# Sliding-window attention and a gated convolution FFN: another order table, batch 0's band masks as TensorE matmuls, conv taps dealt anew

## The chip, the cores and the metric

One core of one Trainium2 chip. The metric is the device time of one execution in microseconds (us), the median of several. Executions of this kernel scatter by 1 to 2%, so each is marked fast or slow (slow: more than 1.5% above the fastest run of the same kernel), and only fast ones are compared. Every ratio below is the mean time of one kernel's fast runs over the mean of the other's fast runs in the same rounds on the same chip, with a 95% interval; it is therefore not quite the ratio of the quoted medians. "Points" are per cent of the time before in such a ratio. A profile is one execution, and its span is some 2 us shorter than the time of the same execution.

## The reference, cut to what matters

```python
# q, k, v: (8 batches, 8 heads, 576 positions, 64)
scores = scale * q @ k.T                    # only |i - j| <= 32 counts
attn = softmax(where(mask, scores, -1e9)) @ v
x = attn.transpose(0, 2, 1, 3).reshape(8, 576, 512)
h = maximum(x @ w_in, 0)                    # 512 -> 1024
conv_out = sum(conv_w[k] * shifted(h, k) for k in range(3))   # along the sequence
out = (h * sigmoid(conv_out)) @ w_out       # 1024 -> 512
```

## The kernel before

The program first writes down all its operations, each with what it reads, writes and which buffers it uses. A table, made by a planner, then fixes in which order they are emitted and on which engine. In `1863S` the number is the operation, the letter the engine: P TensorE, V VectorE, S ScalarE, G GpSimd, D the sync queue, Q ScalarE's own DMA queue; digits behind it choose buffers, and `2F` is two filler matmuls. **Every engine works through its part of the table in order**: if one entry waits, all later entries of the same engine wait.

```python
BUFS = {'st': 3, 'qkb': 5, ..., 'xn': 3, ..., 'y': 7}
CONV = ('33333333', '33q3323r23223321', ...)      # who does the three taps of each unit
ORDER = """15D 11D0 12D 1F 17D ..."""             # 1616 entries
...
def load_v(b, c):                                  # one block of v, 192 or 256 KB, f32
    loader[e].dma_start(vst[..., c, :, :], v[b, :, s0:s1, :]...)
def cast_v(b, c):                                  # to bf16, by V, S or G
    copy(e, ve_b[b % 2][:, c, :, 0:64], vst[:, c, :, :])
...
def emit_exp(e_): scalar.activation(at_..., ps..., AF.Exp, scale=scale)
def emit_mask(e_): (vector if e_ == "V" else gpsimd).tensor_tensor(   # attn * mask
    out=at_..., in0=at_..., in1=mask, op=ALU.mult)
...
# normalised output -> transposed tile, by a transposing transfer ("xd") or by TensorE
loader[e_].dma_start_transpose(to, xn.ap[:, c]...)
```

The parts meet like this: load q, k, v; cast to bf16; transposes and scores on TensorE; exponentials on ScalarE; masks; value products; normalisation; transposed again; first projection (`ph`), relu, three taps, tanh, gate, second projection (`py`), copy `y`, store. Names such as "v 7 4" mean block 4 of v of batch 7.

The softmax here doesn't subtract the row's maximum and nothing guards it: scores larger than these inputs give would overflow.

## Time and profile before

| | before |
|---|---|
| time, median of 3 runs (lowest to highest) | 228.39 us (228.12 to 232.81) |
| span of the profile | 225.6 us |
| TensorE / VectorE / ScalarE / GpSimd busy | 94 / 87 / 83 / 61% |
| mean wait of a transposing transfer from ready to issued | 3.5 us |

TensorE is the bound; how its time adds up is in the prediction. Columns: engine, tile and line, what ended the wait; total us, times, longest.

```profile
POOL ve L232 <- DMA vst<-in_v_dram: 5.8, 6, 1.8
...
ACT ve L232 <- DMA vst<-in_v_dram: 0.7, 1, 0.7
```

These are casts of v that reached the head of their engine's queue before the block had landed. GpSimd (POOL), the engine with the most time to spare, does almost all of that waiting; ScalarE (ACT) waits once, 0.7 us.

### The profile page before, as it was taken

The page shows a single profiled execution, that of the slowest core. Times are in us where ns is not written, and L with a number is a line of the kernel's source. Part 1 is how long each engine was busy: PE and PEld are TensorE (multiplying, and loading weights), DVE is VectorE, ACT ScalarE, POOL GpSimd, SP SyncE. Part 2 cuts the span into 40 slices and gives each one's busy share as a digit, 9 for nine tenths or more (in the row PEclk, how much of TensorE's full clock was granted, in tenths as well). Part 3 has the DMA queues.
Part 4 walks back from the last instruction along what each step waited for, and adds up shares of the span by engine and source line. Part 5 has one row for each costly group of instructions (what it writes and reads, how often), then busy time and mean ns, then how long its engine had stood idle before and what let it go on. Part 6 is the DMA issues. An engine that isn't in the chain of part 4 may idle for free.

```text
span 225.6 us, 7189 instructions
## 1 busy us (share of the span) xinstructions
PE 211.5 (94%) x2720; PEld 122.9 (54%) x2720; DVE 197.3 (87%) x467; ACT 187.5 (83%) x474; POOL 137.7 (61%) x203
## 2 busy tenths in 40 slices
PE   7698899989989999989999998999999999999993
PEld 5366567658555655545555454545655565455541
DVE  6279869899999979797999788989999999899990
ACT  2689899998989889879889989689989999777642
POOL 5978654654376937695368736756386735566640
PEclk9889999999999999999999999999999999999999
DMA  6999999999989999999997989994535212501224
GB/s 201 331 285 358 355 266 281 321 308 253 290 170 324 317 175 287 236 306 224 288 347 129 202 278 358 182 231 147 144 36 118 99 46 49 175 1 49 93 101 178
DMA packets 66391, 48.16 MB, mean 214 GB/s; under 512 B 50781, under 2 KB 50805, under 8 KB 66357
## 3 DMA queue, kind: packets, MB, share of 16 engines
q1 hardware_dynamic: 64992, 46.32, 78.6%
q10 hardware_dynamic: 1364, 1.39, 2.9%
q8 instruction: 21, 0.34, 0.8%
q14 instruction: 14, 0.11, 0.2%
HBM read 32.52 MB, written 9.44 MB: 186 GB/s over the span
## 4 chain that ended last, share of the span: by engine, by line
PE 41%; DVE 18%; ACT 17%; DMA 13%; issue 5%; SPq 3%; POOL 2%; DVEq 0%; ACTq 0%; POOLq 0%
PE pf L232 41%; DMA st<-in_k_dram 7%; ACT attn L232 6%; DVE pf L232 5%; DVE gT L232 4%; SPq L232 3%; DMA out_dram<-y 3%; ACT xn L232 3%; DVE qkT L232 2%; ACT pf L232 2%; DMA vo<-ve 2%; DVE attn L232 2%; DVE xn L232 2%; ACT qkb L232 2%; ACT y L232 1%
## 5 line engine op out<-in xcount | busy, mean ns | idle before, releaser
L232 PE MATMUL pf<-xT,w_in_sb 128*128 128x385 bf16 (+2 forms) x416 | 73.4, 315 | 3.6 <-ACT hT L232 0.9
L232 PE MATMUL pf<-w_out_sb,gT 128*128 128x512 bf16 x288 | 72.2, 380 | 0.0
L232 POOL TENSOR_SCALAR cp<-hT,conv_w_sb 128x384 f32<-128x384 bf16 (+1 forms) x63 | 38.9, 622 | 46.1 <-ACT hT L232 20.2
L232 ACT ACTIVATE pf<-pf 128x384 f32<-128x384 f32 (+1 forms) x104 | 48.2, 477 | 13.1 <-DVE pf L232 11.1
L232 DVE SCALAR_TENSOR_TENSOR gT<-pf,hT 128x384 bf16<-128x384 f32 (+1 forms) x104 | 52.1, 517 | 5.5 <-ACT pf L232 5.1
L232 PEld LDWEIGHTS <-w_in_sb 128*128 128x128 bf16 x416 | 38.6, 98 | 27.8 <-issue 4.5
L232 ACT ACTIVATE attn<-pf 128x512 bf16<-128x512 f32 (+1 forms) x96 | 41.4, 522 | 1.8 <-PE pf L232 1.8
L232 ACT ACTIVATE hT<-pf 128x385 bf16<-128x385 f32 (+2 forms) x76 | 35.4, 487 | 6.0 <-PE pf L232 5.6
L232 PEld LDWEIGHTS <-gT 128*128 128x128 bf16 x288 | 26.0, 98 | 25.7 <-DVE gT L232 0.5
L232 DVE SCALAR_TENSOR_TENSOR pf<-hT,conv_w_sb,pf 128x384 f32<-128x384 bf16 (+1 forms) x61 | 34.7, 586 | 1.2 <-PE pf L232 1.1
L232 PE MATMUL pf<-hT,diag_w 128*128 128x384 bf16 (+1 forms) x153 | 30.9, 309 | 0.9 <-DVE xn L232 0.6
L232 POOL TENSOR_SCALAR qkb<-st 128x1152 bf16<-128x1152 f32 (+1 forms) x23 | 25.7, 1122 | 7.6 <-DMA st<-in_k_dram 3.2
L232 DVE COPY qkT<-pf 128x576 bf16<-128x576 bf16 x35 | 25.6, 750 | 4.9 <-PE pf L232 4.9
L232 POOL TENSOR_TENSOR cp<-cp,cp 128x384 f32<-128x384 f32 (+1 forms) x24 | 24.4, 1016 | 1.6
L232 DVE TENSOR_TENSOR attn<-attn,mask 128x1152 bf16<-128x1152 bf16 x26 | 23.0, 886 | 2.4 <-ACT attn L232 2.3
L232 ACT ACTIVATE xn<-pf,rec 128x64 bf16<-128x64 f32 x96 | 22.0, 360 | 1.5 <-DVE rec L232 1.5
L232 ACT COPY y<-pf 128x512 f32<-128x512 f32 x30 | 18.1, 605 | 3.9 <-PE pf L232 3.7
L232 DVE SCALAR_TENSOR_TENSOR pf<-hT,conv_w_sb,cp 128x384 f32<-128x384 bf16 (+1 forms) x35 | 21.2, 618 | 0.0
L232 POOL TENSOR_TENSOR attn<-attn,mask 128x1152 bf16<-128x1152 bf16 x6 | 14.2, 2371 | 8.4 <-ACT attn L232 8.4
L232 DVE TENSOR_TENSOR xn<-pf,rec 128x256 bf16<-128x256 f32 x48 | 18.9, 410 | 0.0
L232 ACT COPY qkT<-pf 128x576 bf16<-128x576 bf16 x29 | 18.6, 664 | 0.4 <-PE pf L232 0.2
L232 PEld LDWEIGHTS <-diag_w 128*128 128x128 bf16 x153 | 13.3, 97 | 9.8 <-issue 1.3
(49 smaller groups left out, 235.2 us busy)
## 6 DMA issues: line engine op xcount, KB each, us to landing
st<-in_q_dram SPq DMA_DIRECT2D x16, 576.0 KB, 6.8
out_dram<-y SPq DMA_DIRECT2D x36, 256.0 KB, 3.8
st<-in_k_dram SPq DMA_DIRECT2D x14, 576.0 KB, 8.2
vst<-in_v_dram SPq DMA_DIRECT2D x24, 256.0 KB, 7.0
vst<-in_v_dram SPq DMA_DIRECT2D x15, 192.0 KB, 5.7
vo<-ve SPq DMA_DIRECT2D x11, 260.0 KB, 5.6
st<-in_moe_w_in_dram SPq DMA_DIRECT2D x2, 1024.0 KB, 9.3
st<-in_moe_w_out_dram SPq DMA_DIRECT2D x2, 1024.0 KB, 9.4
```

The costliest lines, as they stand in the source:

```text
L232: return lambda *args, **kwargs: fixed(do(*args, **kwargs))
```

## The change

It means to plan the order with an honest issue time for transposing transfers, to take batch 0's masks off the path that starts the FFN (a large negative number is added outside the band by TensorE before the scores accumulate, so that the exponential gives 0), and to deal conv taps and other work to the engines anew.

```diff
+SPLIT = (1,)
-BUFS = {'st': 3, 'qkb': 5, ... 'xn': 3, 'hT0': 8, 'hT1': 6, ... 'gT': 4, 'y': 7}
+BUFS = {'st': 4, 'qkb': 6, ... 'xn': 2, 'hT0': 5, 'hT1': 8, ... 'gT': 3, 'y': 4}
-TURNS = (..., 'edddd')
+TURNS = (..., 'deddd')
+MASKS = ('aa', 'mm', 'mm', 'mm', 'mm', 'mm', 'mm', 'mm')
-CONV = ('33333333', '33q3323r23223321', 's222r32q', ...)
+CONV = ('33333333', '33q3323r23223322', 's222r32r', ...)
-ORDER = """15D 11D0 12D ...          (1616 entries)
+ORDER = """17D 11D0 12D ...          (1607 entries, all drawn anew)
...
+                if added:
+                    for n, e, width in ((2, x, 2), (0, 0, 8), (1, 1, 8)):
+                        rows = slice(64 * e, 64 * e + 64)
+                        tensor.matmul(ps[n].ap[...], outside[rows, :],
+                            ident[rows, None, rows].broadcast_to([64, width, 64]), start=True, stop=False)
...
-                        start=True, stop=True,
+                        start=not added, stop=not (added and more),
```

## The prediction

> **What bounds the kernel now.** I read the busy shares first, then the chain that ended last in order of time, then the busy time by stretch, then TensorE's and the DMA queue's own timelines.
>
> ```profile
> PE 211.5 (94%) x2720; PEld 122.9 (54%) x2720; DVE 197.3 (87%) x467; ACT 187.5 (83%) x474; POOL 137.7 (61%) x203
> ...
> 25.80 7.68 PE pf L232 x93
> ...
> 136.25 48.21 PE pf L232 x603
> ...
> 191.53 2.44 DMA xT<-xn
> 194.01 27.28 PE pf L232 x142
> ```
>
> TensorE is the busiest, VectorE and ScalarE close behind. The real work starts at 25.80 us: the first input projection (`ph`), once batch 0's attention is finished; before that TensorE runs fillers. Two long pieces of the chain are TensorE alone; between 34 and 130 us it changes hands.
>
> ```profile
> 25.80:60.00 34.20, 33.23 (x491) 22.81 (x492) 30.45 (x78) 32.05 (x88) 16.45 (x23) 1.00 1.13 299
> 60.00:110.00 50.00, 47.80 (x764) 26.82 (x763) 45.06 (x105) 44.16 (x110) 34.39 (x32) 1.00 1.08 248
> 110.00:140.00 30.00, 28.12 (x347) 15.78 (x346) 26.96 (x67) 27.08 (x71) 19.61 (x25) 1.00 1.01 275
> 140.00:185.00 45.00, 45.00 (x571) 24.48 (x571) 43.86 (x95) 38.91 (x97) 28.56 (x35) 1.00 0.60 132
> ```
>
> The columns are TensorE, its weight loads, VectorE, ScalarE, GpSimd. TensorE has idle time until 140 us and none from 140 to 185. Its busy time overstates its work[...], so I sum floors, from the step from one start to the next within a group: 0.164 us for 385 columns, 0.163 for 384, 0.216 for 512, and per group 0.36 for 18 transposes, 0.39 for 18 score and 0.13 for 8 value matmuls, 0.22 for a transposed block. After 25.80 that makes 58.1 (88 whole units) + 5.3 (16 half units) + 62.2 (288 output matmuls) + 22.1 (diagonal taps) + 9.7 + 10.9 + 8.2 + 2.2 = **178.7 us**. The stretch from 25.80 to the last matmul's end at 221.7 is 195.9 us, so **about 17 us** are waits and switches. Then 3.9 us for the last copy and store. Span: 25.8 + 178.7 + 17.2 + 3.9 = 225.6; the timed median is 2.8 us more.
>
> ```profile
> 137.80 9.16 SPq L232 DMA_TRANSPOSE xT<-xn  x6
> ...
> 164.67 6.08 SPq L232 DMA_TRANSPOSE xT<-xn  x4
> ...
> 186.20 6.55 SPq L232 DMA_TRANSPOSE xT<-xn  x5
> ```
>
> This is the sync queue's issue time: a transposing transfer holds it 1.3 to 1.5 us in a burst (29 of them sum to 43.6 us, mean 1.50, longest 3.3), an ordinary one 0.5 (median of 120).
>
> [...]
> - [...] 1.5 us of issue against 3.6 us median to landing. That supports planning with a longer issue.
> [...]
>
> **The change, part by part.**
>
> *Batch 0's masks.* Four multiplications leave VectorE and its path. The two that count:
>
> ```profile
> 19.38 0.76 DVE L232 TENSOR_TENSOR attn<-attn,mask 128x1152 bf16<-128x1152 bf16 x1 [0.38 <-ACT attn L232]
> ...
> 20.81 0.74 DVE L232 TENSOR_TENSOR attn<-attn,mask 128x1152 bf16<-128x1152 bf16 x1
> ```
>
> The last value matmuls wait until 21.55, though the last exponential ended at about 19.5: a 2 us path. In their place come 12 mask matmuls, 4 x (2 x 0.216 + 0.056) = 2.0 us, where TensorE would run fillers. But the head is re-dealt too: the taps' diagonal matrices, 8 us on GpSimd, go mostly to VectorE (18 products at about 0.15 us, estimated from the 0.193 us mask copy of that size: 2.7); ScalarE gets the first casts of q and k; batch 0's normalisations all go to VectorE (four left ScalarE, which took 0.8 us each, for 0.33). Walking ScalarE's new queue with measured steps (cast 0.52 or 0.63, eviction 0.53, exponential 0.48 or 0.16; k of batch 0 landing at 8.5 and the second k at 12.55 as before): first scores start at 13.15 instead of 11.4, since the second q's casts now go ahead of them; exponentials end at 19.8. From there VectorE runs 4 reciprocals, 6 products of 0.33, one copy, two block copies of 0.60, to 24.3; the last transposed block and its copy by ScalarE end at 25.4. First projection at **25.45, gain 0.35 us**: of the masks' 2 us most is given back by later scores and a longer VectorE queue.
>
> *Conv kinds.* Diagonal taps on TensorE go from 118 whole + 35 half to 121 + 36: +3 x 0.163 + 0.083 = **+0.6 us** of the bound. GpSimd loses four tap products and two sums (4.8 us), which it had to spare. So this moves work to the bound and gains nothing by count.
>
> *The rest of the deal after the first projection*, count times step: VectorE 171.2 to 174.3 us (+4 relu 1.9, +4 output copies 2.4, +2 block copies 1.2, +3 casts 1.4, -5 q/k evictions 3.3 and small ones); ScalarE 159.2 to 158.8; GpSimd 118.9 to 113.0. VectorE's margin under TensorE shrinks from 7.5 to 5.0 us. Up to chunk 1's last output, ScalarE is dealt 45.9 us against 43.1 before and TensorE's 44.5 in both: that early stretch is ScalarE's.
>
> *Transposing transfers.* In the old order batches 6 and 7 issue them in pairs with no TensorE work between; measured in TensorE work, 11 of 28 steps are under 1.2 us, though each takes 1.5. In the new order 6 are. What it can win directly is small:
>
> ```profile
> who waited for it (us, times):
> ...
>   PE pf L232: 0.8, 2
> ```
>
> These are waits on the transposed tile, 0.5 of them on a transfer. At 192.5 TensorE lost 0.66 us before chunk 10. Indirectly a queue that runs late delays loads and v's shifted copies; at 87.0 TensorE lost 0.5 us for one of those, and the chain passes through the sync queue at 79 to 83 and 107 to 110. The gaps of TensorE over 0.3 us after 25.8 sum to some 6.7 us, most behind VectorE or ScalarE. I choose 0.7 directly and 1.5 indirectly, including what better placed loads (four staging buffers, not three) bring: **-2.2 us**, my softest number.
>
> Sum: -0.35 + 0.6 - 2.2 = -1.95. 228.39 - 1.95 = **226.4 us**.
>
> **The rivals.**
> - *Hidden anyway.* TensorE's waits lie with VectorE and ScalarE, not with transfers: only 0.5 us of its idle time is put to a transposing one. Then the new order brings the head alone and pays 0.6: about 228.5.
> - *Another bound.* The early stretch is ScalarE-bound by 1.4 us of load and VectorE has 3.1 us more overall. If that comes out in full: 229 to 230. For it: both ran 90 to 100% busy from 40 to 75 us. Against: totals still lie below TensorE's.
> - *A new wait for buffers.* Output buffers go from 7 to 4 and the shortest distance between a store and the buffer's next use falls from 11.5 to 5.0 us of TensorE work, where a store needs 0.5 to issue and 3.8 to land; normalised-output buffers go from 3 to 2. If a store sits behind a burst of transposes, a copy waits, holds its bank, and TensorE stops: +1 to +2.
> - *The plan fits much better.* An order whose planned times hold lets fewer waits pile up. If it cures 5 of the 17 us: about 223.
>
> **Range and chances.** The 17 us cap the gain; a 2% gain (under 223.9) needs 4.2 us or more out of it beyond the head and the taps. A 2% loss (over 233) needs two bad rivals together. Predicted 226.4, range 222.8 to 229.6; faster 0.16, same 0.79, slower 0.05.
>
> **What would show it.** First projection between 25 and 26 us (later than 26.5: the head's walk is wrong). TensorE floors after it 179.3 us, so waits and switches of about 15: this is the step that decides. The transposing issues in bursts of six gone, sync-queue waits on TensorE's path at 79 and 107 us gone. ScalarE ahead of VectorE in the chain up to 75 us. No idle ScalarE or VectorE before an output copy on account of a store; if there is, the buffers are the new wait. The prediction fails if waits fall below 12 us, or rise above 18.

The steps are measured in the trace before: from one start to the next 0.216 us at 512 columns, 0.164 at 385, 0.163 at 384 and 0.056 at 128. A 512-column matmul's record lasts 0.380 us on average; that is how far busy time is from the step.

## The result, and the profile after

| | before | after |
|---|---|---|
| time, median of 4 runs each | 228.25 us | 238.12 us |
| ratio of fast runs | | 1.0456 (1.0410 to 1.0502) |
| span of the profile | 225.6 us | 237.6 us |
| first projection starts | 25.80 us | 27.39 us |
| transposing transfer, mean from ready to issued | 3.5 us | 5.8 us |

It is slower by 4.6%, where 0.9% faster was predicted. The chain that ended last, in order of time (start, us, what):

```profile
27.39 7.00 PE pf L233 x72
...
91.50 10.13 DMA vst<-in_v_dram
...
106.25 4.14 DMA xT<-xn
...
139.36 11.49 DMA vst<-in_v_dram
...
151.40 0.64 ACT qkT L233
152.08 39.72 PE pf L233 x447
```

TensorE's unbroken stretch begins at 152 us; it began at 136 before. What stands in front of it are transfers: two blocks of v, 10.1 and 11.5 us each from issue to landing, and one transposed block. Next, busy time in three stretches of 10 us, after and then before (TensorE, weight loads, VectorE, ScalarE, GpSimd, then granted TensorE clock, share of the DMA engines, GB/s):

```profile
100.00:110.00 10.00, 7.17 (x143) 3.94 (x140) 6.12 (x11) 7.75 (x18) 7.90 (x6) 1.00 0.59 133
140.00:150.00 10.00, 7.16 (x75) 3.95 (x71) 8.64 (x21) 5.75 (x18) 7.14 (x8) 1.00 1.12 290
150.00:160.00 10.00, 7.92 (x58) 3.32 (x58) 5.33 (x12) 6.28 (x14) 1.67 (x3) 0.66 0.72 130
```

```profile
100.00:110.00 10.00, 10.00 (x191) 5.59 (x192) 8.05 (x18) 9.47 (x27) 4.60 (x4) 1.00 1.24 223
140.00:150.00 10.00, 10.00 (x98) 4.73 (x96) 9.90 (x19) 7.43 (x16) 8.33 (x11) 1.00 1.19 204
150.00:160.00 10.00, 10.00 (x131) 5.84 (x131) 9.36 (x23) 9.14 (x23) 5.84 (x7) 1.00 0.55 154
```

Where 10.00 stood, 7 to 8 stand, and the clock is 0.66 in the last. To see exactly where the loss is made, I counted the TensorE work not yet begun at a time, with the floors that the prediction lists:

| us from the start | 30 | 100 | 110 | 130 | 140 | 150 | 160 | 180 |
|---|---|---|---|---|---|---|---|---|
| before, us of work left | 174.3 | 113.7 | 104.3 | 86.9 | 77.9 | 69.0 | 59.3 | 39.9 |
| after, us of work left | 176.2 | 113.3 | 107.3 | 91.2 | 82.9 | 76.4 | 71.2 | 52.3 |
| after minus before | 1.9 | -0.4 | 3.0 | 4.3 | 5.0 | 7.4 | 11.9 | 12.4 |

The later start costs nothing in the end: at 100 us the changed kernel is level. **All of the 12 us are lost between 100 and 160 us.** The two largest losses are at 100 to 110 and 140 to 160. ScalarE's timeline there (start, us, engine, line, operation, tiles, count, wait before it and what ended it):

```profile
145.65 0.52 ACT L233 ACTIVATE hT<-pf 128x385 bf16<-128x385 f32 x1
150.87 0.62 ACT L233 CAST ve<-vst 128x512 bf16<-128x512 f32 x1 [4.70 <-DMA vst<-in_v_dram]
151.40 0.63 ACT L233 COPY qkT<-pf 128x576 bf16<-128x576 bf16 x1
```

And TensorE's in the same place:

```profile
145.23 1.03 PE L233 MATMUL pf<-w_out_sb,gT 128*128 128x512 bf16 x4
...
146.76 0.81 PE L233 MATMUL pf<-hT,diag_w 128*128 128x384 bf16 x4
152.08 1.87 PE L233 MATMUL pf<-w_out_sb,gT 128*128 128x512 bf16 x4 [4.51 <-ACT qkT L233]
153.74 1.49 PE L233 MATMUL pf<-xT,w_in_sb 128*128 128x385 bf16 x4
155.03 3.04 PE L233 MATMUL pf<-w_out_sb,gT 128*128 128x512 bf16 x8
```

Read them together. ScalarE stands 4.70 us at the cast of v 7 4. The next entry of its queue is a copy out of a bank (one of the 8 buffers `pf` that TensorE writes into) that TensorE needs, so TensorE stands 4.51 us. Nobody needs that v block yet: its batch comes last. And TensorE comes back slow: four matmuls of 512 columns took 1.87 us where they took 1.03 just before. The other such cast, v 5 0, held ScalarE 2.22 us until 101.65. Both are in the waits:

```profile
POOL ve L233 <- DMA vst<-in_v_dram: 9.7, 8, 2.5
...
ACT ve L233 <- DMA vst<-in_v_dram: 6.9, 2, 4.7
...
PE pf L233 <- ACT qkT L233: 4.5, 1, 4.5
...
DVE y L233 <- DMA out_dram<-y: 2.1, 2, 1.6
```

ScalarE's waits for v went from 0.7 to 6.9 us. In the kernel before, **both of these casts are on GpSimd**. (In all, ScalarE casts 8 blocks of v in place of 12; only these two make it wait.) The lead, TensorE work planned between a load and its cast, is the same: 6.1 us for v 5 0 and 5.8 us for v 7 4 before, 6.4 and 5.9 after. But v 7 4 took 6.5 us from issue to landing before and 11.5 after; the four q and k loads of batch 7 (576 KB each) are issued at 135.7 to 137.3 us, 2 to 4 us ahead of it, where they had 8 to 11 us of lead before. The sync queue's issues in the changed kernel (start, us held):

```profile
135.69 0.43 SPq L233 DMA_DIRECT2D st<-in_q_dram  x1
...
137.25 0.47 SPq L233 DMA_DIRECT2D st<-in_k_dram  x1
...
139.29 3.80 SPq L233 DMA_DIRECT2D vo<-ve  x1
...
143.92 10.73 SPq L233 DMA_TRANSPOSE xT<-xn  x5
```

One ordinary issue, at 139.29 us with six transfers issued and not yet landed, held the queue 3.80 us (the kernel before has one of 3.70 us, at 132.82), and five transposing ones of batch 5 still come in one burst of 10.73 us. The block v 7 4 itself is issued from ScalarE's own DMA queue, at 139.36 us, in both kernels at about the same time (139.96 before).

### The profile page after: what moved, and what is told of

The parts are those of the page before. It is cut to its first block, busy times and chain, and to the rows that moved or that the text cites. A ratio compares the mean times of both kernels' runs of the same rounds, so it can differ in the third digit from the quotient of the medians.

```text
span 237.6 us, 7185 instructions
## 1 busy us (share of the span) xinstructions
PE 216.9 (91%) x2730; PEld 123.8 (52%) x2730; DVE 204.2 (86%) x489; ACT 185.0 (78%) x459; POOL 126.2 (53%) x181
## 4 chain that ended last, share of the span: by engine, by line
PE 48%; DMA 18%; DVE 16%; ACT 9%; issue 5%; SPq 2%; POOL 0%; DVEq 0%; ACTq 0%; POOLq 0%
PE pf L233 48%; DMA vst<-in_v_dram 13%; DVE pf L233 4%; DVE gT L233 3%; DMA st<-in_k_dram 3%; ACT attn L233 2%; DVE xn L233 2%; SPq L233 2%; ACT pf L233 2%; DMA xT<-xn 2%; DVE qkT L233 2%; ACT hT L233 1%; DVE attn L233 1%; ACT qkT L233 1%; DVE rec L233 1%
## 5 line engine op out<-in xcount | busy, mean ns | idle before, releaser
L233 PE MATMUL pf<-xT,w_in_sb 128*128 128x385 bf16 (+2 forms) x416 | 75.1, 317 | 4.1 <-DVE gT L233 1.5
L233 ACT ACTIVATE pf<-pf 128x384 f32<-128x384 f32 (+1 forms) x104 | 47.9, 479 | 13.1 <-DVE pf L233 10.7
L233 POOL TENSOR_SCALAR qkb<-st 128x1152 bf16<-128x1152 f32 x18 | 21.7, 1207 | 19.5 <-DMA st<-in_k_dram 9.7
L233 DVE COPY qkT<-pf 128x576 bf16<-128x576 bf16 x30 | 22.3, 748 | 3.9 <-PE pf L233 2.8
L233 POOL TENSOR_SCALAR ve<-vst 128x512 bf16<-128x512 f32 x24 | 15.9, 669 | 15.1 <-DMA vst<-in_v_dram 9.7
L233 ACT COPY qkT<-pf 128x576 bf16<-128x576 bf16 x34 | 21.3, 660 | 2.2 <-PE pf L233 2.2
L233 POOL TENSOR_TENSOR cp<-cp,cp 128x384 f32<-128x384 f32 (+1 forms) x22 | 21.9, 994 | 1.7
L233 ACT ACTIVATE xn<-pf,rec 128x64 bf16<-128x64 f32 x84 | 19.4, 330 | 3.7 <-DVE rec L233 3.5
L233 ACT COPY y<-pf 128x512 f32<-128x512 f32 x26 | 15.6, 604 | 6.1 <-PE pf L233 6.1
L233 ACT CAST qkb<-st 128x1152 bf16<-128x1152 f32 (+2 forms) x16 | 14.9, 946 | 5.9 <-DMA st<-in_q_dram 4.5
L233 DVE TENSOR_TENSOR attn<-attn,mask 128x1152 bf16<-128x1152 bf16 x22 | 18.1, 826 | 1.5 <-ACT attn L233 1.5
```

The costliest lines, as they stand in the source:

```text
L233: return lambda *args, **kwargs: fixed(do(*args, **kwargs))
```

## The experiments

Seventeen kernels ran, all with correct results. Theory A: ScalarE standing before two late v blocks is the cause. Theory B: TensorE's slow clock after its own wait adds to it. Theory C: places of the transposing transfers. Theories D and E: how transfers queue. Rivals from before: the output buffers, the masks. An edit in the table is shown as a diff of entries; entries between are cut.

### 1. Both casts later in ScalarE's order, and each alone

```diff
-1792P63 1168D 1863S 987V1 ... 1946D 2629S 1706V7
+1792P63 1168D 987V1 ... 1946D 1706V7
+1889S 1372P 1871S 1863S ... 2111G10 2079S 2629S      (v 5 0 later; v 7 4 later)
```

> The changed kernel with two casts of v on ScalarE (batch 5 block 0, batch 7 block 4) moved later in ScalarE's own order, behind 10 and 11 of its other instructions; nothing else differs. Theory A (ScalarE, in order, stands before a cast whose v load has not landed, and TensorE's banks wait behind it): the two waits of 2.2 and 4.7 us go, TensorE's gaps of 2.0 at 100 us and 4.7 at 147 us go, and so does the slow stretch after the second; time 238 falls by 8 to 10, to 228-230. Rival B (the transfers are the limit, the wait only moves to the next user of late data): under 3 us gained, and the same idle time shows on TensorE elsewhere.

> Only the cast of batch 7 block 4 is moved. Theory A: 4.7 us of wait plus about 2.5 us of slow matmuls after it: 6 to 7.5 us faster than the changed kernel, about 231. Rival B: under 2 us.

> Only the cast of batch 5 block 0 is moved. Theory A: the 2.0 us gap of TensorE at 100 us goes, and the late transposing transfer 8 us further on becomes a wait of up to 2 us instead: 1 to 3 us faster than the changed kernel. If it is under 0.5, that transfer was the real limit of this stretch.

| | median | ratio to before |
|---|---|---|
| changed kernel | 238.12 us | 1.0456 (1.0410 to 1.0502) |
| v 7 4 later | 235.09 us | 1.0235 (1.0127 to 1.0342) |
| v 5 0 later | 236.96 us | 1.0440 (1.0354 to 1.0525) |
| both later | 232.34 us | 1.0200 (1.0124 to 1.0277) |

Moving two casts out of 1607 entries gives back 2.6 of the 4.6 points. v 7 4 carries nearly all of that, by its two fast runs (two of its four are slow); v 5 0 alone gives nothing that the intervals tell apart. Theory A had forecast more, 228 to 230 us for both and about 231 for v 7 4 alone: TensorE waits elsewhere instead, in the trace with both later 2.00 and 1.94 us for transposed blocks, where the changed kernel has 1.30. The trace kept of the version with both is of its one slow run (235.91 us); what is read from it below is read with that in mind.

### 2. Keeping TensorE busy in its wait

26 filler matmuls of 256 columns, into a bank that is free there, behind the last tap product before the wait. They change no result and remove no wait.

```diff
-2067G01 1998P2 1715S
+2067G01 1998P2 26H 1715S
+            if engine == "H":
+                for _ in range(int(number)):
+                    filler(1536)
+                continue
```

> The changed kernel with 26 filler matmuls of 256 columns, into a free bank, in TensorE's gap at 147 us. The wait of ScalarE stays. If the granted clock falls because TensorE idles there (0.66 in the window 150 to 160), the next four output matmuls take 1.03 us again, not 1.87, and the kernel is 1.5 to 3 us faster than the changed one. If the slow stretch comes from something else, the same or slower.

Median 236.38 us, ratio 1.0293 (1.0172 to 1.0415, from two fast runs only; its profile is of a slow one). That interval still touches the changed kernel's, so the time alone does not settle theory B; the trace has to. TensorE's timeline in that profile:

```profile
147.05 3.00 PE L236 MATMUL pf<-zero 128*128 128x256 bf16 x26 [0.22 <-DVE qkT L236]
152.33 1.02 PE L236 MATMUL pf<-w_out_sb,gT 128*128 128x512 bf16 x4 [2.28 <-ACT qkT L236]
153.19 0.82 PE L236 MATMUL pf<-xT,w_in_sb 128*128 128x385 bf16 x4
153.84 1.89 PE L236 MATMUL pf<-w_out_sb,gT 128*128 128x512 bf16 x8
```

The wait ends as late as it did (152.33 us, against 152.08 in the changed kernel), but the same three groups take 1.02, 0.82 and 1.89 us in place of 1.87, 1.49 and 3.04: **2.67 us** less, and the granted clock is 1.00 over 150 to 160 us in place of 0.66. In the changed kernel's trace TensorE is idle from 147.57 us, the granted clock is 0.50 from 150.5 to 157.3 us (6.83 us) and 1.00 before and after that, and until then the step at 512 columns is 0.427 us in place of 0.216. So the wait at 147 us cost 4.5 us and then 2.7 more, by the traces.

Shorter waits are less regular: with both casts later, one of 2.00 us at 107 us left the clock at 1.00, while after one of 1.94 us at 154.6 us eight projection matmuls took 2.76 us in place of 1.49 and the clock was 0.83 over 150 to 160. In the trace with the fillers one of 2.28 us left it at 1.00. How long a wait has to be for the clock to fall was not shown.

### 3. The masks alone, in the kernel before

```diff
+ (the kernel before, its own order; `outside`, the added matmuls and the start/stop flags of the
+  change for batch 0; its mask multiplications emit nothing)
```

> The kernel before with one part of the change: batch 0's masks added by TensorE, its four mask multiplications left out, all else in the old order. Theory: first projection 1 to 2 us earlier than 25.8, the time 0.5 to 1.5 us better than before's. If the masks are worth nothing in this order, since the eviction of q and k and the exponentials set the head, within 0.3.

Median 227.16 us, ratio 0.9981 (0.9936 to 1.0025). The masks alone are neither gain nor loss. The first projection did not come 1 to 2 us earlier either: it starts at 26.87 us in this trace, against 25.80 before. (In the traces of the other runs on one and the same head it lies between 26.5 and 28.3 us, so one trace settles it only roughly.)

### 4. Four of the five most delayed transposing transfers earlier; more output buffers

```diff
-1084D ... 1085D ... 1150D ... 1912D          (at their places)
+1083V 1084D 1085D ... 800D 1150D ... 1921D 1912D
```

```diff
-'y': 4
+'y': 6          (and the buffers dealt in turn to six)
```

> The version with both casts moved, and four transposing transfers issued earlier in the sync queue's order: the two of batch 2's last block right after their data is ready (they stood 12 places later, 19 us after it), batch 3 block 0 ahead of four others, batch 5 block 0 ahead of three others. Theory C (what is left is that transposing transfers are issued late, behind a queue that its own transfers block): the gap of 2.1 us before chunk 4's first projection and that of 2.0 us, with slow matmuls after it, before chunk 7's go; 232.3 falls by 3 to 5, to 227.5-229. If TensorE is then held by other late data, the gain is under 1.

> The changed kernel with the four transposing transfers issued earlier, casts left where they are. Theory C with A: the 1.4 us gap before chunk 4 goes, chunk 7 was hidden behind the cast's wait: 1 to 2 us faster than the changed kernel, about 236.5. Rival: freeing the sync queue also lets v loads go earlier and takes part of the casts' waits away: 3 us or more.

> The changed kernel with 6 output buffers in place of 4, taken in turn. The prediction's rival of a new buffer wait: 1 to 2 us faster. What the trace suggests (VectorE waited 2.1 us for stores, beside TensorE's longer waits): under 0.5.

| | median | ratio to before |
|---|---|---|
| both casts later, four transposing transfers earlier | 232.65 us | 1.0197 (1.0148 to 1.0246) |
| four transposing transfers earlier alone | 237.55 us | 1.0452 (1.0402 to 1.0501) |
| six output buffers | 238.37 us | 1.0455 (1.0406 to 1.0503) |

None of the three changes anything against the run that it builds on, although the mean wait of a transposing transfer from ready to issued did fall, from 5.8 to 4.3 us in the first and 4.0 in the second. Theory C falls as a cause that stands alone, and the prediction's buffer rival is out: VectorE's waits for stores, 2.1 us, were not on TensorE's path. The trace of the first of these shows what became of the gain. TensorE's wait of 2.00 us for a transposed block at 107 us is gone, but two of the moved transfers, issued at 79 and 80 us, now stand ahead of two v blocks, which land at 89.3 and 90.4 us in place of 86.3 and 87.2. GpSimd waits 3.21 us for the first of them, and TensorE for the mask that GpSimd computes next but one:

```profile
93.50 0.22 PE L232 MATMUL pf<-ve,attn 128*64 128x65 bf16 x1 [0.86 <-POOL attn L232]
```

So the work left at 110 us is 106.4 us, as much as without the moved transfers (106.2) and 2 us more than in the kernel before; at 130 us it is 90.1, 3 us more. 27 TensorE records are missing from that trace; they are put back in their places here, which is good to about half a microsecond.

### 5. Bulk loads issued sooner

Theory D said that the sync queue, nearly always issuing between 95 and 140 us, starts transfers late. So the eight q and k loads of batches 6 and 7 went to ScalarE's queue, or those of batch 7 went some 7 us earlier.

```diff
-2513D0 ... 2514D ... 2515D1 ... 2516D ... 2612D2 ... 2613D ... 2614D3 ... 2615D
+2513Q0 ... 2514Q ... 2515Q1 ... 2516Q ... 2612Q2 ... 2613Q ... 2614Q3 ... 2615Q     (e7, e8)
+2517D 2612D2 2613D 2614D3 2615D ...                                                  (e9)
```

> The run with both v casts moved, and besides the eight q and k loads of batches 6 and 7 issued from ScalarE's own queue at the same places of the order. Theory D (what is left of the loss, 232.3 against 228.2 us, is the sync queue: it works in order, is nearly always issuing between 95 and 140 us, and so transfers start late): the loads start earlier, about 1 MB of the 1.5 to 2 MB that are missing by 110 to 140 us is made up, and the time falls to 228 to 230.5 us. Rival (the loads' place in the queue is not what is short; the order itself makes TensorE wait, or ScalarE pays as much for eight issues of 0.4 us): 231.5 to 234 us.

> The run with both casts and four transposing transfers moved, and the same eight loads from ScalarE's queue. If sync's queue and the places of the transposing transfers are both needed, as theory D has it: 227.5 to 230 us, the lowest of all the runs on the changed order. Rival: as without the eight loads, 231.5 to 233.5 us.

> The run with both casts moved, and the four q and k loads of batch 7 issued from the sync queue some 7 us earlier (about 128 in place of 135 us, where the kernel before issues them at 129 to 132 us). If those loads standing in the pipe ahead of the v blocks of batch 7 and of batch 5's transposing transfers make the waits of 144 to 160 us: the stretch from 144 to 160 us, which still loses about 4 us to the kernel before, loses under 2, and the time is 229.5 to 231 us. If only the first loss (100 to 125 us) and lateness in general count: 231.5 to 233.5 us.

| | median | ratio to before |
|---|---|---|
| both casts later, eight loads from ScalarE's queue | 238.61 us | 1.0469 (1.0417 to 1.0521) |
| the same and four transposing transfers earlier | 241.08 us | none: three of four runs slow |
| both casts later, batch 7's loads 7 us earlier | 240.38 us | 1.0543 (1.0475 to 1.0612) |

The two that have a ratio gave up the whole 2.6 points: my expectation had the wrong sign. The third, forecast as the lowest of all, has the highest median. The waits of TensorE say why. With the eight loads on ScalarE's queue, then with batch 7's loads earlier, and last the piece of the latter's chain where that happened:

```profile
PE pf L232 <- DMA xT<-xn: 4.7, 1, 4.7
```

```profile
PE pf L232 <- DMA vo<-ve: 6.4, 2, 6.2
```

```profile
132.05 8.51 DMA vo<-ve
```

In the latter, a 260 KB copy that TensorE needs at once was issued behind the four loads of 576 KB and took 8.51 us; in the run with the casts alone the same copy, issued ahead of them, took 4.2, and TensorE did not wait for it. In the former, a transposed block took 6.1 us in place of 3.6, with a 576 KB load issued 0.5 us ahead of it from the other queue. In these two runs the urgent transfer issued behind or beside a bulk load that started sooner took that much longer; how much of it each load causes was not measured, nor does a trace show by what way.

### 6. Bulk loads behind the small ones

```diff
-1696S3 1650V 2615D 1926V ... 2532D 2620Q 1910V1
+1696S3 1650V 1926V ... 2532D 2620Q 2615D 1910V1       (e10, in the changed kernel)
+2532D 2620Q 2614D3 2615D ... 2627G 2623G0 ... 2556S 2624S3     (e11, on the kernel of part 4)
```

> The changed kernel with one issue moved: the last k load of batch 7 (576 KB) is issued right behind the v block 7 4 instead of four transfers ahead of it; ScalarE's order is as in the changed kernel. Theory E ([...]a small urgent transfer pays for every bulk load issued ahead of it; this took the place of theory D, which the runs with earlier bulk loads refuted): the v block lands about 2.5 us sooner, ScalarE's wait before its cast falls from 4.7 to about 2 us, and the time falls by 2 to 4 us to 234 to 236 us. Rival (what counts is only how early or late a transfer is issued): the v block lands at most 0.5 us sooner, the time stays within 1 us of 238.

> The run with both casts and four transposing transfers moved (232.6 us), and besides the second q and k load of batch 7 issued behind the v block 7 4, with their casts later on GpSimd and ScalarE. Theory E: the small transfers of 137 to 150 us land 3 to 5 us sooner after issue, the waits left at 150 us (1.9 us of ScalarE on a k load, 1.25 us of TensorE) go, and the time is 230 to 231.8 us. Rival (what is left is not in the transfers' order at all but in the order of the engines' work): 232 to 234 us.

238.09 us, ratio 1.0463 (1.0374 to 1.0552), and 234.18 us, ratio 1.0231 (1.0065 to 1.0397). Theory E misses in both; the first stays within 1 us of 238 us, as its rival had it, and the second lies just above its rival's 232 to 234. In the first, v 7 4 took 10.7 us in place of 11.5, and ScalarE's wait fell from 4.70 to 3.31 us only, not to 2; ScalarE then waited 2.08 us for the load that was put back. So theory E, that each bulk load ahead costs a small transfer its own time and taking it away gives that back, was too simple. What part 5 measured holds for its two transfers and gives no forecast.

### 7. Only the engine of the two casts

The place in the order stays as the changed kernel has it; the two casts go to GpSimd, where the kernel before has them. Then the same at the later places, then the mirror image: the kernel before, with its two casts on ScalarE.

```diff
-1863S ... 2629S
+1863G ... 2629G          (e12; e13 at the places of part 1; e15 with the four transfers of part 4)
```

```diff
-1843G ... 2601G
+1843S ... 2601S          (e14, in the kernel before)
```

> The changed kernel with the casts of the v blocks 5 0 and 7 4 on GpSimd, as the kernel before has them, at the same places of the order: only the engine of two casts changes. Lead from load to cast is the same in both kernels (6.1 and 5.8 us of TensorE work before, 6.4 and 5.9 after), so if the loss comes from who waits (ScalarE, which stands ahead of TensorE's banks, in place of GpSimd, which waits 46 us beside others anyway), then this brings what the later casts brought: 231.5 to 234.5 us. Rival (a late v block costs as much on GpSimd, whose next work is tap products for VectorE): 236 to 239 us.

> The same two casts on GpSimd and also at their later places. If the wait alone matters, nothing is added to the runs with one of the two: 231.5 to 233 us. If ScalarE's 1.25 us of cast work matters as well: 230 to 231.5 us.

> The kernel before with the casts of v 5 0 and v 7 4 on ScalarE, at their places. In its trace the two blocks landed about 1 us ahead of their casts (at 99.97 and 146.46 us, casts at 100.99 and 147.46 on GpSimd), so ScalarE should wait little. If it takes both, ScalarE and a load that lands late: 228 to 230 us. If ScalarE reaches the casts well before GpSimd did, or any v cast on ScalarE at these places costs: 231 to 234 us.

> The changed kernel with both casts on GpSimd (234.0 us) and the four transposing transfers issued earlier. The trace of the run with the casts alone still loses some 3 us from 100 to 110 us, with TensorE waiting for transposed blocks. If that part is theirs and stays gained: 230.5 to 232 us. If it is lost again later, as it was with the late casts: 233 to 235 us.

| | median | ratio to before |
|---|---|---|
| changed kernel, two casts on GpSimd | 233.98 us | 1.0226 (1.0174 to 1.0278) |
| the same, also later | 234.53 us | 1.0255 (1.0204 to 1.0306) |
| kernel before, its two casts on ScalarE | 228.00 us | 1.0021 (0.9943 to 1.0099) |
| changed, casts on GpSimd, four transfers earlier | 231.95 us | 1.0201 (1.0129 to 1.0274) |

One letter at two of 1607 entries gives back 2.3 points, about as much as the later places did (2.6), and the two together give no more: it is one and the same wait. GpSimd and TensorE in the trace with the casts on GpSimd, then the waits:

```profile
146.99 1.02 PE L232 MATMUL pf<-w_out_sb,gT 128*128 128x512 bf16 x4
...
150.03 0.62 POOL L232 TENSOR_SCALAR ve<-vst 128x512 bf16<-128x512 f32 x1 [4.25 <-DMA vst<-in_v_dram]
```

```profile
POOL ve L232 <- DMA vst<-in_v_dram: 16.3, 9, 4.3
...
PE pf L232 <- POOL qkb L232: 1.4, 1, 1.4
```

The block is as late as ever, GpSimd waits 4.25 us for it, and TensorE runs straight on. GpSimd's waits for v sum to 16.3 us, nearly three times those of the kernel before, and the kernel is 2.3 points faster than with ScalarE waiting 6.9. But GpSimd is not free everywhere. At v 5 0 the move gains little: TensorE, which had waited 1.85 us at 103 us behind ScalarE, now waits 1.45 us for a cast of q that stands on GpSimd directly behind the cast of v 5 0. And in part 4 a wait of GpSimd for v reached TensorE. How free a wait is depends on the entries behind it, on GpSimd too.

The mirror image costs nothing: in the kernel before, the blocks land before ScalarE reaches them. These are ScalarE's two casts in that trace, without a wait:

```profile
101.82 0.66 ACT L230 CAST ve<-vst 128x512 bf16<-128x512 f32 x1
...
149.02 0.61 ACT L230 CAST ve<-vst 128x512 bf16<-128x512 f32 x1
```

So here it took both: a block that lands late, and an engine in front of the path that waits for it. Four transfers earlier on top (231.95 us, 1.0201) are within the interval of the casts alone. Their trace, with its missing records put back, has 104.6 us of work left at 110 us, level with the kernel before (104.3), where the casts alone have 106.6; from there to 160 us it loses 3.6 us to the kernel before, the casts alone 4.1. By the traces the moved transfers gain some 2 us here, and the time lies in the range forecast for that (230.5 to 232); by the ratios the gain is not shown.

## Why the prediction was wrong

The step that failed is the third term of the sum, "Transposing transfers ... **-2.2 us**, my softest number", and with it the step that the prediction called decisive, "waits and switches of about 15". They came to 27 us: 237.6 (span) - 27.39 (first projection) - 179.3 (floors) - 3.9 (tail) = 27.0. Point by point:

- **Floors +0.6 us, tail 3.9 us:** the tail holds (last matmul's end at 233.7, span 237.6); the floors are counts of instructions, and the table of work left uses them.
- **Head, 25.45 us:** wrong, 27.39. k of batch 0 landed at 8.98 us where I had let it land at 8.5; the first scores started at 14.7 us, not 13.15, the exponentials ended at 20.6, not 19.8, and from there to the first projection it took 6.8 us, not 5.65. (The diagonal products on VectorE took 4.2 us in all where I had 2.7, by the measure of another instruction; but they were done by 11.8 us, ahead of that path.) This does not explain the loss, because the changed kernel is level at 100 us.
- **Masks alone:** worth nothing measurable (0.9981). The 0.35 us was for the whole new head, so this neither confirms nor refutes it.
- **Signs:** up to 75 us VectorE, not ScalarE, has more of the chain outside TensorE (14.7 against 11.2 us), and sync-queue time is still in the chain at 78 and at 88 to 91 us. A slip in the sums: a 2% gain needs 4.8 us beyond the head and the taps, not 4.2, since the taps' 0.6 us had to be made up as well.
- **Transposing transfers:** "issues in bursts of six gone" did not come: there are five in 10.73 us at 143.92 and six in 8.97 us at 177.07. The sum of their issue time stayed (43.6 and 43.2 us), and from ready to issued they wait 5.8 us in place of 3.5. I counted only how much TensorE work lies between two issues, which got better, and not how late in the sync queue the first one stands. Moving four of the five worst alone changed nothing.
- **"Indirectly a queue that runs late delays loads":** late loads did matter, with the wrong sign. I gave it 1.5 us of gain. Loads stood later in relation to their users than before, v 7 4 for example 11.5 us from issue to landing in place of 6.5; that the late queue made it so was not shown.
- **The rival that was missing:** a late load on another engine. I listed ScalarE as a bound by load and buffers as a wait; I did not ask which engine casts which block; these two casts appear in the prediction only inside the busy totals, "ScalarE 159.2 to 158.8; GpSimd 118.9 to 113.0". Two casts moved from GpSimd, where the wait for v 7 4 cost TensorE nothing, to ScalarE, where it is TensorE's: 2.3 points of 4.6, by the engine alone.
- **"A new wait for buffers":** absent, by the run with six.
- **What capped the loss:** "A 2% loss needs two bad rivals together" took the waits of the trace before as if the new table would inherit them. A new order makes its own waits; the old ones bound the gain, not the loss.

By the trace, the wait before v 7 4 made a second loss that no step had: 2.7 us of slow clock.

**What stays open:** 2.0 to 2.3 points, some 5 us. They are in 100 to 160 us too (in the trace with the casts on GpSimd, work left against the kernel before goes from -0.4 us at 100 to +2.3 at 110, +4.1 at 150 and +6.4 at 160). The transposed blocks that TensorE waits for at 109 us are part of the picture, but moving four of them did not settle it: with the casts on GpSimd it made up the loss to 110 us in the trace, but not clearly in the time, and the loss of some 4 us after 110 us stayed. Buffers, earlier bulk loads and later ones did not settle it either. Whether the rest lies with the deal of VectorE and ScalarE or with transfers as a whole, these runs do not tell. No version ran that beats the kernel before beyond doubt.

## What to carry to other kernels

When a table deals work to engines that run in order, ask of every instruction that waits for a transfer not only whether the data comes in time, but who stands behind it: put such instructions where nothing urgent stands behind them, on another engine or later in the same queue (here 2.3 and 2.6 points of 4.6). A planner that counts busy time alone sees no difference between the two. And when a change redraws an order, judge it by the lead of its loads against the landing times that the trace shows, since the waits of the old trace bound what can be gained, not what can be lost (here 17.2 us before, 27.0 after).
